# Strassen's identity for the second product of a fused attention and feed-forward kernel: seven block products for eight

## The chip, the core and the metric

The kernel runs on one core of a Trainium2 chip. Its five engines run side by side, each through its own queue in order: TensorE (PE, matmuls; its weight loads are listed as PEld), VectorE (DVE), ScalarE (ACT), GpSimd (POOL) and SyncE (SP, which here only issues transfers). TensorE writes to the accumulator memory PSUM, which has eight banks of 128 x 512 fp32 values. GpSimd and the transfers work on SBUF only. The metric is the device time of one execution in microseconds (us); the median of several runs is given. All times below are in us unless marked ns.

## The reference

There are two parts. The first is a cross attention between tokens and states, both ways, for 8 batches, 8 heads, 512 tokens, 32 states and a head width of 64. The second is a feed-forward layer over all 8 x (512 + 32) = 4352 rows, in width 512, hidden width 2048.

```python
scores = scale * np.matmul(x, state.transpose(0, 1, 3, 2))
a = softmax(scores);  xread = np.matmul(a, state)
scores2 = scale * np.matmul(state, x.transpose(0, 1, 3, 2))
a2 = softmax(scores2);  sread = np.matmul(a2, x)
attn = np.concatenate([xread, sread], axis=2)   # heads joined to rows of 512
h = attn @ w_in
g = np.maximum(0.01 * h, h)
out = g @ w_out
```

Inputs and output are fp32; the kernel multiplies in bf16 and adds in fp32.

## The kernel before, in words

The order of the work on every engine is the order of the program: it is written out by hand, with no planner, and each engine's queue runs in that order, held only by waits for data and for free buffers.

The tokens' first product is folded. For a batch, `a_m` multiplies the states with w_in in four column groups of 512 to a matrix M, so that `ff1` gets a block of 128 hidden columns for all 512 tokens from two matmuls (M as weights, the probabilities aT moving, 512 columns). ACT applies the leaky ReLU from one of two PSUM banks ("ph") into hT, which holds 16 blocks of 128 hidden columns by 512 tokens in bf16.

The second product is done in pieces. `piece(b, hT, i, jq)` adds four matmuls (128 tokens by 512 columns of w_out, one weight tile of hT each) to a bank ("py"); four pieces finish 128 tokens, and `y_store` copies the bank to SBUF and issues a transfer of 256 KB.

Batches 0 and 1 have openings of their own. Batches 2 to 7 each have a stage of 16 steps (the loop `for b in range(2, B)`). Step s runs `ff1` for hidden block s, then what the step's branch holds, then one piece: at steps 0 to 9 the rest of batch b - 1, at 10 to 15 the first three quarters of two token tiles of batch b. A matmul of ff1 can start only when the activation two blocks before has left its bank. The branches prepare the next batch, called nxt:

- step 0: SP issues the load of x[b+2] (`load_x`, 1 MB) and the transposition of the state-side probabilities (`a_a2t`).
- step 1: TensorE computes the scores of nxt and M's column group 3 for b. VectorE takes row maxima, spreads them and subtracts (`a_shift`), then column maxima (`a_max2`). Pool casts x[b+2] to bf16 (`cast_x`).
- steps 5 to 7: ACT's exponentials (`a_exp`, `a_exp2`), and VectorE's sums, reciprocals and scalings (`a_probs`, `a_probs2`).
- step 8: the states' read (`a_sread`), which needs the transposition of step 0.
- step 10: M's column groups 0, 2 and 1 of nxt; VectorE evicts 0 and 2, ACT evicts 1.
- step 13: SP issues the transposition of x[b+2] (`a_xt_dma`), which the scores need at step 1 of the next stage.

Stage 2 also loads the states of batches 4 to 7 (`load_state(1)`, step 4) and prepares them (`state_t(1)`, step 8: a cast on Pool, a transposition issued by SP). All of SP's issues are in order: a transfer whose data is late holds those behind it.

PSUM holds two banks each for "ph" and "py", and two double banks, "sc" and "big": "sc" serves scores and an M group, "big" serves M groups and the states' read.

The tail is after stage 7. `ff1_s` computes the hidden rows of the 256 state tokens (four matmuls of 256 columns per block), between the last pieces of batch 7; then come the states' second product (eight pieces) and `last_tile`, the last 128 tokens of batch 7 in two halves of 256 columns. The profile's line numbers are those of the listing below: L346 is ff1, L374 a piece, L357 ff1_s, L400 last_tile, L325 a_m, L204 the scores, L339 and L337 evictions of M, L246 the last product of a_probs, L283 the scaling of a_probs2, L104 the cast of x, L98 its load, L188 and L175 and L290 the transpositions of x, of the states and of a2.

Of the kernel before, what the change touches and what calls it, by code (L numbers as in the profile page):

```python
# [9 lines left out]
P = 128  # L10
B, H, S, D = 8, 8, 512, 64
# [16 lines left out]
def kernel(  # L28
# [14 lines left out]
    att = ctx.enter_context(tc.tile_pool(name="att", bufs=2))  # L43
    mpool = ctx.enter_context(tc.tile_pool(name="mpool", bufs=2))
    hpool = ctx.enter_context(tc.tile_pool(name="hpool", bufs=2))
    ypool = ctx.enter_context(tc.tile_pool(name="ypool", bufs=4))
    psum = ctx.enter_context(tc.tile_pool(name="psum", bufs=2, space=bass.MemoryType.PSUM))

    ENG = mybir.EngineType
# [44 lines left out]
    xs, xl = {}, {}  # L94

    def load_x(b, eng):
        xl[b] = xpool.tile([P, H, NT * D], FP32, name="xl", tag="xl", bufs=2)
        eng.dma_start(xl[b][:], x[b].rearrange("h (p t) d -> p h (t d)", t=NT))  # L98

    def open_xb(b):  # L100
# [2 lines left out]
    def cast_x(b, h0, h1, copy):  # L103
        copy(  # L104
            xs[b][:, :, h0:h1].rearrange("p t h d -> p h t d"),
            xl[b][:, h0:h1].rearrange("p h (t d) -> p h t d", t=NT),
        )
# [110 lines left out]
        return m1  # L218

    def block_sub(flat, m1, n):  # L220
        m1b = att.tile([P, n, NS], FP32, name="mrowb", tag="mrowb")
        nc.vector.transpose(m1b[:], m1[:, :, None].to_broadcast([P, n, NS]))  # L222
        sh = att.tile([P, n * NS], FP32, name="sh", tag="sh")
        nc.vector.tensor_tensor(  # L224
            out=sh[:], in0=flat, in1=m1b[:].rearrange("p c j -> p (c j)"), op=ALU.subtract,
        )
        return sh

    def block_exp(sh, n):
        e1 = att.tile([P, n * NS], BF16, name="e1", tag="e1")  # L230
        nc.scalar.activation(out=e1[:], in_=sh[:], func=AF.Exp, scale=SCALE)  # L231
        return e1

    def block_probs(dst, e1, n):
        r1 = att.tile([P, n], FP32, name="r1", tag="r1")
        nc.vector.tensor_reduce(  # L236
            out=r1[:], in_=e1[:].rearrange("p (c j) -> p c j", j=NS),
            axis=AX.X, op=ALU.add, apply_transpose=True,
        )
        nc.vector.tensor_scalar(out=r1[:], in0=r1[:], scalar1=1e-9, scalar2=None, op0=ALU.add)  # L240
        q1h = att.tile([P, n], BF16, name="qh", tag="qh")
        with nc.allow_low_precision(reason="one rounding, of the finished reciprocal"):
            nc.vector.reciprocal(q1h[:], r1[:])
        q1b = att.tile([P, n, NS], BF16, name="qb", tag="qb")
        nc.vector.transpose(q1b[:], q1h[:, :, None].to_broadcast([P, n, NS]))  # L245
        nc.vector.tensor_tensor(  # L246
            out=dst, in0=e1[:].rearrange("p (g s) -> p g s", g=2),
            in1=q1b[:].rearrange("p (g c) j -> p g (c j)", g=2), op=ALU.mult,
        )
# [38 lines left out]
    def a_a2t(a):  # L288
        a.a2T = att.tile([P, 2, NT, P], BF16, name="a2T", tag="a2T")
        nc.sync.dma_start_transpose(  # L290
            a.a2T[:].rearrange("p g i q -> p (g i) q"), a.a2[:].rearrange("p g s -> p (g s)")
        )

    def a_sread(a):
        ps = psum.tile([P, NK, 2, NS], FP32, name="psr", tag="big", bufs=1)
        for k in range(NK):
            for i in range(NT):
                nc.tensor.matmul(  # L298
                    ps[:, k, :, :],
                    lhsT=a.xb[:, i, 2 * k:2 * k + 2, :].rearrange("p h d -> p (h d)"),  # L300
                    rhs=a.a2T[:, :, i, NS * k:NS * (k + 1)],
                    start=(i == 0), stop=(i == NT - 1),
                )
        for g in range(2):
            nc.scalar.copy(
                sr_t[D * g:D * (g + 1), :, NS * a.b:NS * (a.b + 1)],
                ps[D * g:D * (g + 1), :, g, :],
            )
# [72 lines left out]
    def y_store(b, i, copy):  # L381
# [6 lines left out]
        else:  # L388
            nc.sync.dma_start(rows_of(b)[i], ysb[:])

    def rows_of(b):
        return out[b * SROW:b * SROW + S, :].rearrange("(p t) f -> t p f", t=NT)

    def last_tile(b, hT, i):
        n = DM // 2
        for half, copy in ((0, VEC), (1, SCA)):
            cols = slice(n * half, n * (half + 1))
            py = psum.tile([P, n], FP32, name="pyh", tag="py")
            for j in range(16):
                nc.tensor.matmul(  # L400
                    py[:], lhsT=hT[:, j, P * i:P * (i + 1)], rhs=w_out_bf[:, j, cols],
                    start=(j == 0), stop=(j == 15),
                )
            ysb = ypool.tile([P, n], FP32, name="ysh", tag="ysb")
            copy(ysb[:], py[:])  # L405
            nc.sync.dma_start(rows_of(b)[i][:, cols], ysb[:])

    att_of = [Attn() for _ in range(B)]
    a0, a1, a2 = att_of[:3]
# [249 lines left out]
    for s in range(16):  # L663
        ff1(a1, h1, s)
        if s % 2:
            pb, hT, i, jq = fill[s // 2]
            piece(pb, hT, i, jq, copy=VEC if s == 3 else SCA)
        if s == 4:
            a_scores(a2)
            m_evict(a2, 0, a_m(a2, 0, "big"), SCA)  # L670
            a_shift(a2)
            a_max2(a2)
        elif s == 7:
            a_exp(a2)
            a_open(att_of[3], 3)
            a_xt_dma(att_of[3])
        elif s == 8:
            a_sread(a0)
        elif s in (9, 11):
            a_exp2(a2, s // 2 - 4)  # L680
            if s == 9:
                a_probs(a2)
            else:
                a_probs2(a2)
        elif s == 13:
            a_probs2(a1)
            a_a2t(a1)
            pm = [a_m(a2, 1, "big"), a_m(a2, 2, "sc")]
            m_evict(a2, 1, pm[0], VEC)
            m_evict(a2, 2, pm[1], SCA)  # L690

    h_prev = h1
    for b in range(2, B):
        hT = hpool.tile([P, 16, S], BF16, name="hT", tag="hT")
        a = att_of[b]
        nxt = att_of[b + 1] if b + 1 < B else None
        order = [(b - 1, i, 3) for i in range(2)]
        order += [(b - 1, i, jq) for i in range(2, NT) for jq in range(4)]  # L700
        order += [(b, i, jq) for jq in range(3) for i in range(2)]
        for s in range(16):
            ff1(a, hT, s)
            if s == 0:
                if b + 2 < B:
                    load_x(b + 2, nc.sync)
                    open_xb(b + 2)
                a_a2t(a)
            elif s == 1:
                if nxt is not None:  # L710
                    a_scores(nxt)
                m_evict(a, 3, a_m(a, 3, "big"), SCA)
                if nxt is not None:
                    a_shift(nxt)
                    a_max2(nxt)
                if b + 2 < B:
                    cast_x(b + 2, 0, 8, POO)
            elif s == 4:
                if b == 2:
                    load_state(1)  # L720
            elif s == 6:
                if b == 2:
                    a_sread(a1)
            elif s == 8:
                a_sread(a)
                if b == 2:
                    state_t(1)
            if nxt is not None:
                if s == 5:
                    a_exp(nxt)  # L730
                elif s in (6, 7):
                    a_exp2(nxt, s - 6)
                    if s == 7:
                        a_probs(nxt)
                        a_probs2(nxt)
                elif s == 10:
                    pm0 = a_m(nxt, 0, "big")
                    pm2 = a_m(nxt, 2, "phpy")
                    pm1 = a_m(nxt, 1, "sc")
                    m_evict(nxt, 2, pm2, VEC)  # L740
                    m_evict(nxt, 0, pm0, VEC)
                    m_evict(nxt, 1, pm1, SCA)
                if s == 13 and b + 2 < B:
                    a_open(att_of[b + 2], b + 2)
                    a_xt_dma(att_of[b + 2])
            pb, i, jq = order[s]
            piece(pb, hT if pb == b else h_prev, i, jq)
        h_prev = hT

    hs = hpool.tile([P, 16, B * NS], BF16, name="hs", tag="hs", bufs=1)
    b = B - 1
    order = [(0, 3), (1, 3), (2, 0), (2, 1), (2, 2), (2, 3)]
    for s in range(8):
        ff1_s(hs, 2 * s)
        ff1_s(hs, 2 * s + 1)
        if s < 6:
            piece(b, h_prev, *order[s])
        else:  # L760
            piece(B, hs, 0, s - 6)
    for jq in range(2, 4):
        piece(B, hs, 0, jq)
    for jq in range(4):
        piece(B, hs, 1, jq)
    last_tile(b, h_prev, 3)


# [28 lines left out]
```

## Time and profile before

| what | value |
|---|---|
| median of 3 runs | 219.07 us (219.03 to 219.18) |
| span of the profiled execution, first to last instruction | 216.9 us |
| the profiled execution's own time | not listed; span and median differ by 2.17 us |
| granted TensorE clock | 1.000 in the mean |
| busy: PE, ACT, DVE, POOL | 96%, 63%, 46%, 10% of the span |
| transfers | 27.70 MB, of which 17.30 read and 8.91 written in main memory |
| the costliest group: pieces of tokens (L374) | 443 matmuls, 379 ns each as listed |

Three things help in reading it. The duration listed for one matmul includes its passage through the array, and matmuls overlap, so the rate is read from the distance between starts. A group's line gives the line, the engine, the operation, output and inputs by the program's names, shapes, count, then busy time and the mean of one, then the idle time of that engine just before it and what ended it. The timeline lists start, duration, engine and operation, with neighbours of one kind merged.

The stages, by the first matmul of ff1 in the timeline: batch 2 from 54.75 us, 3 from 77.94, 4 from 100.66, 5 from 123.38, 6 from 146.10, 7 from 168.84, the tail from 190.48; the last matmul ends at 213.2. TensorE is busy in nearly every moment of these stages. Stage 2 is longer than the others by one states' read (of batch 1), stage 7 shorter, since it has no next batch. VectorE is busy 12.0 us of a stage, ACT 15.7, Pool 1.9.

### The profile page before, as it was taken

What the parts mean: (1) busy time and instruction counts of PE and PEld (TensorE: products, weight loads), DVE (VectorE), ACT (ScalarE), POOL (GpSimd) and SP (SyncE); (2) the same over time, 40 slices, a digit from 0 to 9 for tenths busy, and PEclk for the clock granted to TensorE, in tenths of its full rate; (3) what the DMA queues carried; (4) which work ended last, traced back from release to release, by engine and by line L of the source; (5) the groups of instructions that cost most, each with busy time, mean ns of one, the idle gap of its engine ahead of it and who ended that gap; (6) DMA issues with size and microseconds to landing.
All of it is one profiled execution on the core that took longest, in us unless ns stands there. A gap on an engine that the chain in (4) does not pass through costs nothing.

```text
span 216.9 us, 3693 instructions
## 1 busy us (share of the span) xinstructions
PE 207.3 (96%) x1481; PEld 98.0 (45%) x1508; DVE 99.3 (46%) x153; ACT 136.8 (63%) x259; POOL 22.8 (10%) x38
## 2 busy tenths in 40 slices
PE   7899999969999999999999999999999999999993
PEld 2543434334454444444454445444444445466562
DVE  1768598698466427840966086706672000000000
ACT  3469566768868566865696478747784756464320
POOL 8830002030031002001200030000000000000000
PEclk9999999999999999999999999999999999999999
DMA  5999993993892992179214851352012110111122
GB/s 176 224 206 290 208 285 68 223 301 73 229 200 81 159 252 76 51 160 227 97 51 114 234 138 53 83 110 100 34 60 51 51 62 35 48 51 48 48 62 87
DMA packets 39888, 27.70 MB, mean 128 GB/s; under 512 B 24512, under 2 KB 35136, under 8 KB 39872
## 3 DMA queue, kind: packets, MB, share of 16 engines
q1 hardware_dynamic: 34944, 21.04, 38.3%
q0 software_dynamic: 4784, 6.29, 14.3%
q8 instruction: 12, 0.20, 0.4%
q10 hardware_dynamic: 144, 0.13, 0.4%
q14 instruction: 4, 0.03, 0.1%
HBM read 17.30 MB, written 8.91 MB: 121 GB/s over the span
## 4 chain that ended last, share of the span: by engine, by line
PE 92%; DMA 3%; DVE 2%; issue 1%; ACT 1%; ACTq 0%
PE py L374 49%; PE ph L346 21%; PE pm L325 4%; PE ph L357 3%; DMA a2T<-a 3%; PE pyw L374 3%; PE pspin L131 2%; PE ph L572 2%; PE psr L298 2%; PE pyh L400 2%; PE sc L204 1%; PE php L572 1%; DVE M L339 1%; ACT xT L435 1%; PE pxth L428 1%
## 5 line engine op out<-in xcount | busy, mean ns | idle before, releaser
L374 PE MATMUL py<-w_out_bf,hT 128*128 128x512 bf16 x443 | 116.5, 379 | 1.1
L351 ACT ACTIVATE hT<-ph 128x512 bf16<-128x512 f32 x112 | 66.7, 601 | 41.8 <-PE ph L346 41.8
L374 PEld LDWEIGHTS <-hT 128*128 128x128 bf16 x496 | 46.8, 98 | 57.1 <-issue 5.3
L346 PE MATMUL ph<-aT,M 128*128 128x512 bf16 x223 | 65.6, 379 | 0.1
L346 PEld LDWEIGHTS <-M 128*128 128x128 bf16 x224 | 21.7, 98 | 26.6 <-issue 0.8
L383 ACT COPY ysb<-py 128x512 f32<-128x512 f32 x30 | 17.6, 586 | 10.5 <-PE py L374 10.5
L214 DVE TRANSPOSE_TENSOR_REDUCE mrow<-sc 128x32 f32<-128x1024 f32 x7 | 8.8, 1250 | 33.0 <-PE sc L204 33.0
L405 DVE COPY ysh<-pyh 128x256 f32<-128x256 f32 x1 | 0.4, 425 | 47.7 <-PE pyh L400 47.7
L104 POOL CAST xb<-xl 128x2048 bf16<-128x2048 f32 (+1 forms) x6 | 10.5, 1751 | 79.3 <-DMA xl<-in_x_dram 57.8
L339 ACT CAST M<-pm 128x1024 bf16<-128x1024 f32 x13 | 13.2, 1013 | 1.9 <-PE pm L325 1.5
L236 DVE TRANSPOSE_TENSOR_REDUCE r<-e 128x32 f32<-128x1024 bf16 x7 | 8.7, 1243 | 9.6 <-ACT e L231 9.6
L339 DVE CAST M<-pm 128x1024 bf16<-128x1024 f32 x9 | 11.0, 1217 | 1.5 <-PE pm L325 1.5
L272 ACT ACTIVATE e<-sc,mcols 128x512 bf16<-128x512 f32 x16 | 11.2, 703 | 0.0
L337 DVE CAST M<-pm 128x512 bf16<-128x512 f32 x12 | 7.7, 685 | 6.3 <-PE pm L325 6.3
L264 DVE TENSOR_REDUCE mcol<-sc 128x2 f32<-128x1024 f32 x8 | 9.7, 1214 | 0.0
L361 ACT ACTIVATE hs<-ph 128x256 bf16<-128x256 f32 x16 | 6.0, 384 | 4.6 <-PE ph L357 4.4
L222 DVE STREAM_TRANSPOSE mrowb<-mrow 128x1024 f32<-128x1024 f32 x7 | 8.7, 1246 | 0.2
L245 DVE STREAM_TRANSPOSE qb<-qh 128x1024 bf16<-128x1024 bf16 x7 | 8.7, 1245 | 0.2
L224 DVE TENSOR_TENSOR sh<-sc,mrowb 128x1024 f32<-128x1024 f32 x7 | 8.6, 1224 | 0.2
L357 PE MATMUL ph<-sr_t,w_in_bf 128*128 128x256 bf16 x64 | 8.3, 273 | 0.0
L231 ACT ACTIVATE e<-sh 128x1024 bf16<-128x1024 f32 x7 | 7.4, 1050 | 1.1 <-DVE sh L224 1.1
L580 ACT ACTIVATE hT<-ph 128x512 bf16<-128x512 f32 x12 | 6.4, 598 | 2.1 <-PE ph L572 1.8
(97 smaller groups left out, 154.2 us busy)
## 6 DMA issues: line engine op xcount, KB each, us to landing
out_dram<-ysb SPq DMA_DIRECT2D x31, 256.0 KB, 2.3
xl<-in_x_dram SPq DMA_DIRECT2D x5, 1024.0 KB, 6.5
w_in_bf<-in_moe_w_in_dram POOLq DMA_DIRECT2D x4, 512.0 KB, 9.3
w_out_bf<-in_moe_w_out_dram POOLq DMA_DIRECT2D x4, 512.0 KB, 16.9
xf<-in_x_dram SPq DMA_DIRECT2D x2, 512.0 KB, 5.1
x<-in_x_dram POOLq DMA_DIRECT2D x2, 512.0 KB, 14.0
xl<-in_x_dram POOLq DMA_DIRECT2D x1, 1024.0 KB, 18.8
out_dram<-ysb SPq DMA_DIRECT2D x8, 64.0 KB, 1.7
```

What stands on the lines that cost most here:

```text
L104: copy(xs[b][:, :, h0:h1].rearrange("p t h d -> p h t d"), xl[b][:, h0:h1].rearrange("p h (t d) -> p h t d", t=NT),)
L214: nc.vector.tensor_reduce(out=m1[:], in_=flat.rearrange("p (c j) -> p c j", j=NS), axis=AX.X, op=ALU.max, apply_transpose=True,)
L222: nc.vector.transpose(m1b[:], m1[:, :, None].to_broadcast([P, n, NS]))
L236: nc.vector.tensor_reduce(out=r1[:], in_=e1[:].rearrange("p (c j) -> p c j", j=NS), axis=AX.X, op=ALU.add, apply_transpose=True,)
L264: nc.vector.tensor_reduce(out=m2[:], in_=a.sc[:], axis=AX.X, op=ALU.max, negate=True)
L272: nc.scalar.activation(out=a.e2[:, g], in_=a.sc[:, g, :], func=AF.Exp, bias=a.m2s[:, g:g + 1], scale=SCALE, accum_out=a.r2[:, g:g + 1],)
L339: copy(a.M[:, :, cols], pm[:])
L346: nc.tensor.matmul(ph[:], lhsT=a.M[:, g, P * j:P * (j + 1)], rhs=a.aT[:, g, :], start=(g == 0), stop=(g == 1),)
L351: nc.scalar.activation(out=hT[:, j, :], in_=ph[:], func=AF.Prelu, alpha=0.01)
L357: nc.tensor.matmul(ph[:, :n], lhsT=w_in_bf[:, k, P * j:P * (j + 1)], rhs=sr_t[:, k, :], start=(k == 0), stop=(k == NK - 1),)
L374: nc.tensor.matmul(y.py, lhsT=hT[:, j, P * i:P * (i + 1)], rhs=w_out_bf[:, j, :], start=(j == 0), stop=(j == 15),)
L383: copy(ysb[:], ys[b, i].py)
```

## The change

The second product of batches 2 to 7, and that of the state tokens, is cut into 2 by 2 blocks. The tokens of a batch are split in two halves of 256, the hidden width in even and odd blocks of 128 (k), and the output columns in two halves of 256. Strassen's identity (in Winograd's form) then needs seven block products in place of eight. Products 1 and 2 use blocks of hT and w_out as they are; 3 to 7 use sums of blocks on one side or both.

- Four sums of blocks of w_out ("tw") are made once, in bf16, on Pool: eight operations of 4 x 256 elements per partition with two inputs each. The first four come in batch 1's stage after step 8, the second four at step 1 of stage 2, behind the cast of x[4]. Their tiles take over the space of the first loads of x.
- Four sums of blocks of hT ("su") are made per batch on DVE, 8 x 256 elements per partition each: sums 0 and 1 in two halves (step 11 of the batch's own stage, step 0 of the next), 2 at step 3 and 3 at step 6.
- A unit is two matmuls of 128 tokens by 256 columns. A product is eight units, a batch 56. The ten first units are run at the end of a batch's own stage (OWN), 46 in the next: three or four a step.
- Products share two banks. 1, 6 and 7 add up in one; 2 is alone in the other; 5 and 3 add up there after it; 4 is alone in the first. ACT saves the bank after 1, 6, 5 and 7 (128 x 512, fp32). DVE joins: an output quarter is the bank plus a saved one, after 2, 3 and 4. Pool adds the saved 7 and 5 for the fourth.
- The output goes out in two transfers of 512 KB per batch, each of 2 rows (4 KB) per partition, after the joins of 3 and 4.
- Column maxima (a_max2) move from step 1 to step 3. M's column group 2 moves from step 10 to step 13, from the banks "ph" and "py" to "big", and its eviction from DVE (two of 512) to ACT (one of 1024).
- To make room, xl (the landing buffer of x) goes from two buffers to one, and so do mrowb, sh, e1 and qb; ysb goes from four to three. The state tokens' hidden rows hs take a buffer of hT.
- The tail runs ff1_s with one or two units of batch 7 at each block, then the seven products of the state tokens (units of one matmul), with up to four units of batch 7 after each of the first six. The state tokens' product 4 is last; its two halves of rows go out in four transfers each (out_s).

```diff
+    def weights_sums(m0, m1):
+        ms = slice(m0, m1)
+        for dst, u, v, op in (
+            (0, B12, B11, ALU.subtract), (2, B22, B12, ALU.add),
+            (1, B11, tw[2], ALU.subtract), (3, tw[1], B21, ALU.add),
+        ):
+            nc.gpsimd.tensor_tensor(
+                out=tw[dst][:, ms], in0=u[:, ms], in1=v[:, ms], op=op
+            )
...
+        def sums(self, n, m0=0, m1=NM, eng=None):
...
+            u, v, op = (
+                (A[2, 1], A[2, 2], ALU.subtract), (S[0], A[1, 1], ALU.subtract),
+                (A[2, 1], A[1, 1], ALU.subtract), (A[1, 2], S.get(1), ALU.add),
+            )[n]
...
+                (eng or nc.vector).tensor_tensor(out=S[n][:, ms], in0=u[:, ms], in1=v[:, ms], op=op)
...
+        def unit(self, bank, n, m, first):
...
+            for i in range(self.sub):
+                nc.tensor.matmul(
+                    bank[:, i, :], lhsT=lhs[:, m, P * i:P * (i + 1)], rhs=rhs[:, m, :],
+                    start=(first and m == 0 and i == 0), stop=(m == NM - 1),
...
+        def done(self, n, bank):
+            f = self.f
+            if n in (1, 6, 5, 7):
+                f.save(n, bank)
+            if n == 2:
+                f.join(self.yo(0)[:, :, :HC], bank, 1)
+            elif n == 7:
+                nc.gpsimd.tensor_tensor(
+                    out=self.yo(1)[:, :, HC:], in0=f.sv[7][:], in1=f.sv[5][:], op=ALU.add
+                )
+            elif n == 3:
+                f.join(self.yo(0)[:, :, HC:], bank, 6)
+                self.out(0)
+            elif n == 4:
+                f.join(self.yo(1)[:, :, :HC], bank, 7)
+                self.out(1)
...
         elif s == 8:
             a_sread(a0)
+            weights_open()
+            weights_sums(0, 4)
...
                 a_a2t(a)
+                if before:
+                    for n in (0, 1):
+                        before.f.sums(n, 4, 8)
             elif s == 1:
                 if nxt is not None:
                     a_scores(nxt)
                 m_evict(a, 3, a_m(a, 3, "big"), SCA)
                 if nxt is not None:
                     a_shift(nxt)
-                    a_max2(nxt)
                 if b + 2 < B:
                     cast_x(b + 2, 0, 8, POO)
+                if b == 2:
+                    weights_sums(4, 8)
+            elif s == 3:
+                if before:
+                    before.f.sums(2)
+                if nxt is not None:
+                    a_max2(nxt)
...
+            if s == 11:
+                for n in (0, 1):
+                    now.f.sums(n, 0, 4)
...
-                    pm2 = a_m(nxt, 2, "phpy")
                     pm1 = a_m(nxt, 1, "sc")
-                    m_evict(nxt, 2, pm2, VEC)
                     m_evict(nxt, 0, pm0, VEC)
                     m_evict(nxt, 1, pm1, SCA)
+                elif s == 13:
+                    m_evict(nxt, 2, a_m(nxt, 2, "big"), SCA)
...
-            piece(pb, hT if pb == b else h_prev, i, jq)
...
+            n = 3 + s % 2 if b > 2 else 2
+            left = len(before.units) if before else 0
+            if left:
+                before.run(min(n, left))
+            if n > left:
+                now.run(min(n - left, OWN - own))
```

## The prediction

> **What bounds the kernel now.** I read the shares of busy time first, then the chain that ended last, then the timeline of each engine around one batch.
>
> ```profile
> PE 207.3 (96%) x1481; PEld 98.0 (45%) x1508; DVE 99.3 (46%) x153; ACT 136.8 (63%) x259; POOL 22.8 (10%) x38
> ...
> PE 92%; DMA 3%; DVE 2%; issue 1%; ACT 1%; ACTq 0%
> ```
>
> TensorE is busy 96% and is 92% of the chain: in the stages of batches 2 to 7 it never waits, so time comes off only where TensorE has less to do, and every new wait of TensorE is paid in full. The end of the chain in order of time (start, duration) gives the price of a narrow matmul, and the timeline that of a wide one:
>
> ```profile
> 202.80 0.87 PE ph L357 x8
> ...
> 209.71 3.51 PE pyh L400 x32
> ```
> ```profile
> 185.73 1.03 PE L374 MATMUL py<-w_out_bf,hT 128*128 128x512 bf16 x4
> 186.59 0.59 PE L346 MATMUL ph<-aT,M 128*128 128x512 bf16 x2
> ```
>
> Eight of 256 columns take 0.87, 32 take 3.51: 0.109 each, a new weight tile with each. Four of 512 take 186.59 - 185.73 = 0.86: 0.2155 each. Rates of the other engines (min/median/max ns, and groups with mean ns):
>
> ```profile
> L104 POOL CAST xb<-xl x6: 1040/1893/1894, 34.5 to 125.7; 128x2048 bf16<-128x2048 f32 x5, 128x1024 bf16<-128x1024 f32 x1
> ```
> ```profile
> L111 DVE CAST xb<-xf x2: 427/618/808, 5.4 to 7.0; 128x512 bf16<-128x512 f32 x2
> ...
> L111 POOL CAST xb<-xf x1: 609/609/609, 7.0 to 7.0; 128x512 bf16<-128x512 f32 x1
> ```
> ```profile
> L246 DVE TENSOR_TENSOR aT<-e,qb 128x1024 bf16<-128x1024 bf16 x7 | 4.9, 704 | 0.2
> ...
> L383 DVE COPY ysb<-py 128x512 f32<-128x512 f32 x1 | 0.7, 692 | 1.2 <-PE py L374 1.2
> ```
>
> Pool needs 0.833 ns per element that it reads, and 0.19 more. The same DVE cast took 0.43 alone and 0.81 at 7.03, when Pool's own cast held from 6.95 to 7.56. Last, the queues around batch 2 (SyncE, VectorE, Pool):
>
> ```profile
> 53.30 1.23 SPq L290 DMA_TRANSPOSE a2T<-a  x1
> 54.63 0.53 SPq L98 DMA_DIRECT2D xl<-in_x_dram  x1
> ...
> 67.36 1.19 SPq L175 DMA_TRANSPOSE st_t<-stb  x1
> 70.10 0.36 SPq L389 DMA_DIRECT2D out_dram<-ysb  x1
> 70.52 3.67 SPq L188 DMA_TRANSPOSE xT<-xb  x1
> ```
> ```profile
> 49.86 0.69 DVE L246 TENSOR_TENSOR aT<-e,qb 128x1024 bf16<-128x1024 bf16 x1
> ...
> 53.19 1.22 DVE L339 CAST M<-pm 128x1024 bf16<-128x1024 f32 x1
> ```
> ```profile
> 62.12 1.89 POOL L104 CAST xb<-xl 128x2048 bf16<-128x2048 f32 x1 [15.73 <-DMA xl<-in_x_dram]
> 66.72 0.61 POOL L174 CAST stb<-stf 128x512 bf16<-128x512 f32 x1 [2.72 <-DMA stf<-in_state_dram]
> ```
>
> SyncE issues in order: the state's transposition waits for Pool's cast of it, and the transposition of x[4] stands behind that.
>
> **The sum's base.** The profiled execution has a span of 216.9; the median of the three runs is 219.07, so 2.17 lies around the span. I keep that and add changes to 219.07.
>
> **TensorE's work.** A batch's second product was 64 x 0.2155 = 13.79; seven products of 8 x 2 narrow matmuls are 112 x 0.109 = 12.21. Batch 2's stage (54.75 to 77.94) held 16 pieces; now 10 pieces and 20 narrow matmuls, 8.62 + 2.18: -2.99. In the stages of 3 to 6: -1.58 each. M's column group 2 goes to a place of its own at step 13, one more gap of 0.09 as before the other group starts: batch 2 -2.90, 3 to 6 -1.49 x 4 = -5.96, batch 7 -1.58. The tail held 64 narrow (6.98), 6 pieces (5.17), 8 pieces of the states (6.90) and 32 narrow (3.49), 22.54; now 6.98 + 92 x 0.109 (10.03) + 56 x 0.109 (6.10) = 23.11: +0.57. Sum -9.87.
>
> **DVE in the stages of 3 to 6.** It was busy 12.0 of 22.7. Out: two copies of M, 1.37. In: sums of 4 x 1024 and 2 x 2048 bf16 elements, by L246 (start to start 0.61, and twice the elements 1.14) 4.7; three joins of 512 at 0.69, 2.1. Some 17.5 of a stage of 21.2: it fits on average, so what counts is order. Let t be 0 at the first matmul of a stage. Scores at step 1 let the row maximum start at t = 2.10 (ff1 of step 1 at 1.09, plus 102.97 - 101.96); the three operations up to the subtraction take 3.70 (102.97 to 106.67). The join of product 2 is queued behind them: 5.80 to 6.49. TensorE reaches product 5, which starts over that bank, at step 4: 5 x 0.431 + 14 units x 0.218 + 0.65 (scores and M) = 5.86. It waits to 6.55: 0.69 in each of four stages, +2.76 (not in batch 7, which has no next batch). Bounds: 0, if the scores' chain starts earlier, and 1.4, if the join costs twice the copy that prices it. Behind it all meets: third sum done at 10.2, needed at 12.2; join 3 at 17.3, needed at 18.8; join 4 at 19.7, needed at 21.0. The halves of sums 0 and 1 at step 0 wait for the last activation and are done by 1.4, ahead of the scores.
>
> **ACT.** Four copies out (0.586), four saves of the same size in, one copy of M (1.01) more: 16.7 of 21.9 busy. Each save has a whole product of 1.7 before its bank is used again: 0. The activations' own reserve is the two banks of ff1, which a late exponential would use up first.
>
> **SyncE and DMA in later stages.** Two outputs of 512 KB for four of 256 KB. The first goes after join 3 (t = 17.3), the transposition of x[b+2] behind it lands 4.8 later (4.3 to 5.8), at 22 to 23.5, needed at 23.5: 0, with almost no reserve. The load of x[b+2], now one buffer, goes behind the second output at about 21, casts by t = 7 of the next stage, needed by step 13: 0. The tiles that go from two buffers to one (row maxima spread, shifted scores, exponentials, reciprocals) are each read within the stage that writes them, the last read by t = 15 and the next write after t = 23: 0.
>
> **The end.** From the last matmul to the end it is 3.7 (213.2 to 216.9), 3.2 of it from the last DMA's issue. Now three groups queue on SyncE: four row DMAs of the first state tile from 0.75 before the last matmul's end (0.42 each, median), batch 7's output (0.35), four more: the last goes at 2.54, so 5.74: +2.0. Bounds 0 and 3.
>
> **The weight sums on Pool, the term that decides.** Eight operations of 1024 elements with two inputs. No such row; bounds are 1.04 (one element per read cycle, the 1024 cast) and two reads, 0.19 + 2 x 0.853 = 1.89. I take 1.89: both inputs must be read. The Trainium skill (GPSIMD Engine Reference, section 3.1) has 4.5 for 2048 elements with two inputs, so an estimate of 2.3 here, and the sum would be some 3 later; no run here shows it.
> The L111 rows say that a DVE operation meeting a Pool operation waits for its end: 0.81 is the rest of Pool's 0.53 plus 0.43, less 0.15. I count that wait as whole, and let the engines alternate. Bounds: nothing, or the whole of the Pool operation each time. The Trainium skill (SBUF - State Buffer, Who interferes with whom) calls it an exclusive lock for the whole instruction, also for DVE operations with two SBUF inputs; by that rule, the trace agrees.
> First four: Pool is free at 46.4 and starts them there. L246 goes from 49.86 to 50.4, the scalings of a2 wait to 53.0 and 55.1, and the cast of M at 53.19 starts at 56.5 and ends at 57.7. Its bank is wanted at 56.79: TensorE waits 1.0. The transposition of a2 (53.30) is issued at 56.6, the load of x[4] behind it at 57.9 instead of 54.63, so Pool's cast moves from 62.12 to 65.4.
> Second four: queued behind that cast, from 67.4, alternating with L240, L246 and the scalings: done at 76.4. The state's cast 77.1, its transposition's issue 78.3, the output 78.7, x[4] lands at 83.5. Scores of batch 4 stand at step 1 of batch 3: 77.94 - 2.90 + 1.60 = 76.64 without any wait. All waits on the way are inside this one: +6.9. The longest wait of TensorE in the trace is 1.7, at a granted clock of 1.00; whether the clock holds over 4 to 5 it does not show, and I price that at 0.
>
> **Sum.** 219.07 - 9.87 + 2.76 + 2.0 + 6.9 = 220.9.
>
> **Rivals.**
> Faster, Pool is quick: at 1.04 the first four are over at 50.8, nothing is late, the second four end at 68.9, x[4] lands at 75.9, before 76.64. Then 214.0. For it: Pool has little else to do. Against: two inputs. It is decided at about 1.7 per operation, where the wait eats the 5.1 gained.
> Faster, no blocking: at 1.89 the second four run from 64.0 to 71.7, x[4] lands at 78.7: +2.1, 216.1. Against: 0.43 to 0.81.
> Slower, DVE is the bound: if the sums, over strided blocks, run at the rate of L224 (1024 in 1.22), each batch gets 4.3 more, 22 of 21.9; join 4 comes after it is wanted, about 1 a stage: 225. Against: L246 also reads two bf16 inputs, in rows of 512.
> The change doesn't do what it says: above 13.79/112 = 0.123 a narrow matmul saves nothing, and it ends near 230. Against: 0.109 in L357 and L400.
>
> **How the numbers follow.** Forecast as worked out 0.58, own range 218.8 (a price near 1.7) to 224 (the end at its bound, +1, and x[b+2] late by 0.5 in four stages, +2); quick Pool 0.13; no blocking 0.17; both faster cases with 1 to either side; DVE bound 0.08; no saving 0.04. Within 0.2% (0.44, what a measurement of this kernel can tell from no change): a band of the forecast's lower end, 0.05. Faster: 0.13 + 0.17 + 0.03 of the forecast's low end = 0.33; slower 0.62. The range 213.5 to 224 leaves out the two last cases and a rest of the first rival.
>
> **What would show it.** Narrow products at 0.109; Pool's sums near 1.9 and DVE operations stretched beside them; a wait of TensorE for the DMA of xT in batch 3 of 3 to 5; four waits of 0.7 for the join at step 4; 5.7 after the last matmul. It is wrong if Pool's sums are near 1, if DVE beside them keeps its durations, or if xT is in time.

## The result: slower by 2.2%

The changed kernel takes 223.98 us (median of 4 runs, 223.65 to 224.14), the kernel before 219.08 on the same chip. The ratio is 1.0221, with a 95% interval of 1.0206 to 1.0236: 4.9 us lost where the forecast lost 1.8. The profiled execution took 223.65 with a span of 221.9, against 216.9 before: 5.0 in span. The chips of the later experiments had the kernel before at 219.1 to 219.2, so their times are compared directly. The ratios leave out a few executions that were over 1.5% slower than the fastest of the same kernel, and they are not formed from the medians, so they can differ by some 0.3% from the quotient of the medians.

The page of the changed kernel, shares of busy time and the chain that ended last:

```profile
PE 202.4 (91%) x1804; PEld 127.3 (57%) x1804; DVE 151.0 (68%) x205; ACT 142.2 (64%) x266; POOL 48.9 (22%) x53
...
PE 44%; DVE 25%; DMA 17%; POOL 5%; issue 5%; SPq 1%; POOLq 0%; DVEq 0%
```

TensorE is busy 4.9 less than before, but it is 44% of the chain and no longer 92%: the other engines and the transfers are now most of it. What TensorE waits for in the changed kernel (total, number of waits, longest):

```profile
PE pm L326 <- DVE M L340: 2.7, 1, 2.7
PE ph L347 <- ACT hT L352: 2.6, 2, 2.1
PE py L375 <- DVE ysb L384: 2.3, 1, 2.3
PE yq L446 <- DVE yo L458: 2.0, 4, 0.5
PE sc L205 <- DMA xT<-xb: 1.5, 3, 0.8
```

By the first matmul of each stage in the two timelines, the 5.0 lie as follows.

| part | before | after | change |
|---|---|---|---|
| ahead of stage 2 | 54.75 | 58.01 | +3.26 |
| stage 2 | 23.19 | 24.54 | +1.35 |
| stages 3 to 6 | 90.90 | 89.82 | -1.08 |
| stage 7 | 21.64 | 20.04 | -1.60 |
| tail, to the end of the last matmul | 22.72 | 23.31 | +0.59 |
| from there to the end | 3.7 | 6.18 | +2.48 |

**Ahead of stage 2**, where nothing was forecast, lie the second and the third line of the waits. The timeline of VectorE, then of TensorE:

```profile
45.29 0.69 DVE L384 COPY ysb<-py 128x512 f32<-128x512 f32 x1 [6.05 <-DMA out_dram<-ysb]
45.90 1.24 DVE L215 TRANSPOSE_TENSOR_REDUCE mrow<-sc 128x32 f32<-128x1024 f32 x1
```
```profile
46.04 1.02 PE L375 MATMUL py<-w_out_bf,hT 128*128 128x512 bf16 x4 [2.32 <-DVE ysb L384]
51.37 0.59 PE L347 MATMUL ph<-aT,M 128*128 128x512 bf16 x2 [2.11 <-ACT hT L352]
```

VectorE is idle for 6.05 ahead of its copy of an output of batch 0, until the transfer of an earlier output has read its buffer: ysb has three buffers where it had four. In the kernel before, the same copy starts at 40.39 after an idle time of 1.24, which TensorE ends. The row maxima of batch 2 queue behind that copy, and TensorE stops for the copied bank and then twice for an activation (2.11, and 0.44 at 52.40). The waits of 1.74 for a2T and of 0.41 for x that the kernel before has in this stretch are gone: 2.32 + 2.11 + 0.44 - 1.74 - 0.41 = 2.72 of the 3.26.

**Stage 2** holds the weight sums. Pool's timeline, then VectorE's:

```profile
68.81 2.12 POOL L410 TENSOR_TENSOR tw_xf<-w_out_bf 128x1024 bf16<-128x1024 bf16 x1
70.89 2.57 POOL L410 TENSOR_TENSOR tw_x<-w_out_bf 128x1024 bf16<-128x1024 bf16 x1
73.54 2.13 POOL L410 TENSOR_TENSOR tw_xf<-w_out_bf,tw_x 128x1024 bf16<-128x1024 bf16 x1
75.74 2.12 POOL L410 TENSOR_TENSOR tw_x<-tw_xf,w_out_bf 128x1024 bf16<-128x1024 bf16 x1
77.80 0.67 POOL L175 CAST stb<-stf 128x512 bf16<-128x512 f32 x1
```
```profile
69.34 1.25 DVE L246 STREAM_TRANSPOSE qb<-qh 128x1024 bf16<-128x1024 bf16 x1
...
71.40 2.08 DVE L279 TENSOR_SCALAR r<-r 128x2 f32<-128x2 f32 x1
...
73.72 4.29 DVE L284 TENSOR_SCALAR a<-e,qc 128x512 bf16<-128x512 bf16 x2
77.93 1.21 DVE L340 CAST M<-pm 128x1024 bf16<-128x1024 f32 x1
```

The same operations 14 to 16 us earlier in the same timeline, with no sum on Pool:

```profile
57.02 0.16 DVE L279 TENSOR_SCALAR r<-r 128x2 f32<-128x2 f32 x1
...
57.42 0.62 DVE L284 TENSOR_SCALAR a<-e,qc 128x512 bf16<-128x512 bf16 x2
```

An operation on two columns that takes 0.16 alone takes 2.08 beside Pool, and two that take 0.62 together take 4.29: each ends within 0.2 of the end of a Pool sum (73.48 and 73.46, 78.01 and 77.86). A transposition of 1024 elements (1.25) beside the sums takes what it takes alone (1.25 at 55.13). The cast of M is queued behind them, so TensorE waits, and then runs slowly. TensorE's timeline, and four windows of 1.2 us (busy time of PE, PEld, DVE, ACT and POOL, then the granted clock, the share of the DMA engines and GB/s):

```profile
79.19 0.63 PE L326 MATMUL pm<-w_in_bf,st_t 64*32 64x512 bf16 x8 [2.67 <-DVE M L340]
85.01 0.41 PE L205 MATMUL sc<-xT,st_t 64*32 64x512 bf16 x8 [0.78 <-DMA xT<-xb]
```
```profile
79.20:80.40 1.20, 1.20 (x12) 0.58 (x12) 1.17 (x2) 0.52 (x1) 0.00 (x0) 0.50 0.53 109
80.40:81.60 1.20, 1.20 (x5) 0.58 (x4) 0.06 (x1) 0.50 (x1) 0.00 (x0) 0.50 0.67 190
81.60:82.80 1.20, 1.20 (x9) 0.71 (x7) 0.00 (x0) 0.64 (x2) 0.00 (x0) 0.86 1.05 209
82.80:84.00 1.20, 1.20 (x10) 0.75 (x8) 0.62 (x1) 1.20 (x3) 0.00 (x0) 1.00 1.12 206
```

For 3 us after the wait the clock is at 0.50 to 0.86 and TensorE does 1.2 x (0.50 + 0.50 + 0.14) = 1.37 less. Wait and clock are 4.0; without them stage 2 is 20.5, 2.7 shorter than before.

**At the end** SyncE still issues for 3.7 after the last matmul's end (215.72). Its timeline:

```profile
214.97 1.75 SPq L918 DMA_DIRECT2D out_dram<-yhs  x4
216.83 0.36 SPq L480 DMA_DIRECT2D out_dram<-yo  x1
217.30 2.12 SPq L918 DMA_DIRECT2D out_dram<-yhs  x4
```

### The profile page after: what moved, and what is told of

The parts are those of the page before. It is cut to its first block, busy times and chain, and to the rows that moved or that the text cites. A ratio compares the mean times of both kernels' runs of the same rounds, so it can differ in the third digit from the quotient of the medians.

```text
span 221.9 us, 4381 instructions
## 1 busy us (share of the span) xinstructions
PE 202.4 (91%) x1804; PEld 127.3 (57%) x1804; DVE 151.0 (68%) x205; ACT 142.2 (64%) x266; POOL 48.9 (22%) x53
## 4 chain that ended last, share of the span: by engine, by line
PE 44%; DVE 25%; DMA 17%; POOL 5%; issue 5%; SPq 1%; POOLq 0%; DVEq 0%
PE yq L446 19%; PE ph L347 8%; DMA xT<-xb 7%; DMA w_in_bf<-in_moe_w_in_dram 5%; PE pyw L375 3%; PE ph L358 3%; DMA out_dram<-ysb 3%; DVE mrowb L223 3%; DVE mrow L215 3%; DMA xl<-in_x_dram 3%; DVE su L435 3%; PE py L375 2%; DVE M L340 2%; POOL tw_xf L410 2%; DVE aT L247 2%
## 5 line engine op out<-in xcount | busy, mean ns | idle before, releaser
L446 PEld LDWEIGHTS <-su 128*128 128x128 bf16 x416 | 40.0, 98 | 16.5 <-issue 4.8
L446 PE MATMUL yq<-tw_xf,su 128*128 128x256 bf16 x192 | 27.6, 272 | 2.0 <-DVE yo L458 2.0
L446 PE MATMUL yq<-w_out_bf,hT 128*128 128x256 bf16 x192 | 27.3, 278 | 0.0
L375 PE MATMUL py<-w_out_bf,hT 128*128 128x512 bf16 x96 | 24.2, 379 | 2.3 <-DVE ysb L384 2.3
L435 DVE TENSOR_TENSOR su<-hT 128x1024 bf16<-128x1024 bf16 (+1 forms) x18 | 16.6, 924 | 12.1 <-ACT hT L352 12.1
L458 DVE TENSOR_TENSOR yo<-yq,sv 128x512 f32<-128x512 f32 x18 | 12.3, 686 | 16.6 <-PE yq L446 16.6
L340 ACT CAST M<-pm 128x1024 bf16<-128x1024 f32 x18 | 18.2, 1011 | 5.0 <-PE pm L326 4.9
L455 ACT COPY sv<-yq 128x512 f32<-128x512 f32 x24 | 14.0, 585 | 3.3 <-PE yq L446 3.2
L446 PE MATMUL yq<-tw_x,hT 128*128 128x256 bf16 x96 | 13.5, 273 | 0.0
L446 PE MATMUL yq<-w_out_bf,su 128*128 128x256 bf16 x96 | 13.5, 273 | 0.0
L446 PE MATMUL yq<-tw_x,su 128*128 128x256 bf16 x96 | 13.4, 273 | 0.0
```

The costliest lines, as they stand in the source:

```text
L340: copy(a.M[:, :, cols], pm[:])
L375: nc.tensor.matmul(y.py, lhsT=hT[:, j, P * i:P * (i + 1)], rhs=w_out_bf[:, j, :], start=(j == 0), stop=(j == 15),)
L435: (eng or nc.vector).tensor_tensor(out=S[n][:, ms], in0=u[:, ms], in1=v[:, ms], op=op)
L446: nc.tensor.matmul(bank[:, i, :], lhsT=lhs[:, m, P * i:P * (i + 1)], rhs=rhs[:, m, :], start=(first and m == 0 and i == 0), stop=(m == NM ...
L455: copy(t[:], bank)
L458: nc.vector.tensor_tensor(out=dst, in0=bank, in1=self.sv[n][:], op=ALU.add)
```

## The experiments

Two causes were in question: Pool's sums, as forecast, and the buffer taken from ysb, which the forecast had not priced. The first runs ask whether both carry a share (A), or the buffer (B) or the sums (C) carry it alone. The edits below are to the changed kernel where nothing else is said.

**1. A fourth place for batch 0's outputs.** The second output tile of batch 0 goes to the space of the later output tile yo0.

```diff
+        if (b, i) == (0, 1):
+            ysb = ypool.tile([P, 2, DM], FP32, name="yo0", tag="yo0", bufs=1)[:, 0, :]
+        else:
+            ysb = ypool.tile([P, DM], FP32, name="ysb", tag="ysb")[:]
...
```

> The second output tile of batch 0 gets a buffer of its own, so that three ysb buffers do what four did; all else as changed. Theory A (two causes, each hiding a part of the other: the wait of DVE's copy for an output transfer, 6.05, and Pool's sums that block DVE and hold up the transposition of x[4]): TensorE's waits of 2.3 and 2.1 in batch 1's stage go, but Pool's first four sums, 2.12 each, then hold DVE's scalings and the cast of M instead; scores of batch 4 come about 2 earlier: 222.0. Theory B (the buffer alone): the whole 8.3 by which the scores of batch 4 are late goes: 215.7. Theory C (Pool's sums alone): 224.0, no change.

Measured: 221.01 (220.97 to 221.70), ratio to the kernel before 1.0077 [1.0028, 1.0126]. The buffer is worth 3.0 us, 1.0 more than theory A expected. TensorE no longer waits for ysb. What remains is the wait for M in two places (1.28 at the start of stage 2, 2.70 at its end), and the wait for a2T is back:

```profile
PE pm L326 <- DVE M L340: 4.0, 2, 2.7
...
PE psr L299 <- DMA a2T<-a: 1.8, 1, 1.8
```

**2. The weight sums on VectorE**, all eight, in the same places of the order.

```diff
-            nc.gpsimd.tensor_tensor(
-                out=tw[dst][:, ms], in0=u[:, ms], in1=v[:, ms], op=op
-            )
+            with nc.allow_low_precision(reason="operands of a product"):
+                nc.vector.tensor_tensor(
+                    out=tw[dst][:, ms], in0=u[:, ms], in1=v[:, ms], op=op
+                )
```

> All eight weight sums on DVE, at the same places of the program, in place of Pool; three ysb buffers as changed. Each should take 0.7 on DVE. Theory A: the wait for the output transfer stays, stage 2 still begins at 58.0, but then runs without waits of TensorE for M and for x[4] and without the half clock after them: scores of batch 4 near 80.2 instead of 85.0: 219.2. Theory B: 224 or more, as DVE has 5 more to do. Theory C: 215.7.

Measured: 220.04 (218.68 to 222.22, 10 runs), ratio 1.0041 [1.0013, 1.0068]; 3.9 less than the changed kernel. Each sum takes 0.69 on VectorE. The wait for M is gone, the wait of 2.5 for ysb stands, and so does the one of 2.1 for an activation behind it.

**3. Both.**

> Both: the second output tile of batch 0 in a buffer of its own, and the eight weight sums on DVE. Theory A: stage 2 begins near 54.8, the scores of batch 4 stand near 76.8: 215.7, with the later stages and the tail as changed. Theory B or C alone: the same 215.7, reached by one of the two edits. Rival D (the seven products do not pay on TensorE, the waits are only where the loss shows): 219 or above.

Measured: 216.25 (214.38 to 216.89), ratio 0.985 [0.9796, 0.9904]. The two causes add up within the spread of the runs (3.0 + 3.9 = 6.9, against 7.7 for both), and the kernel is now faster than before: both causes are real, and nearly apart from each other. That a VectorE too full is behind this loss is excluded, since it carries more work here than in the changed kernel. VectorE's timeline shows one sum that still meets Pool's cast of x, then Pool's:

```profile
62.84 0.68 DVE L414 TENSOR_TENSOR tw_x<-w_out_bf 128x1024 bf16<-128x1024 bf16 x1
63.55 2.38 DVE L414 TENSOR_TENSOR tw_xf<-w_out_bf,tw_x 128x1024 bf16<-128x1024 bf16 x1
```
```profile
63.50 1.89 POOL L105 CAST xb<-xl 128x2048 bf16<-128x2048 f32 x1 [17.22 <-DMA xl<-in_x_dram]
```

The cast begins 0.05 earlier and ends at 65.39; the sum ends 0.54 after it. Alone it takes 0.69, so at most 0.15 of it was done while Pool ran.

**4. Pool's order.** The second four sums go behind the state cast, from step 1 to step 8 of stage 2. This parts two effects of the sums: the queue on Pool in front of the state cast (and so of x[4]'s transposition), and the blocking of VectorE.

```diff
-                if b == 2:
-                    weights_sums(4, 8)
             elif s == 3:
...
                     state_t(1)
+                    weights_sums(4, 8)
```

> Pool's second four weight sums are put behind the cast of the states of batches 4 to 7 (step 8 instead of step 1 of stage 2), still on Pool; all else as changed. If what counts is SyncE's queue (x[4]'s transposition behind the states' behind Pool's sums): scores of batch 4 no longer wait for x[4], and the half clock may still come: about 222.5. If what counts is DVE blocked by Pool (scalings, then the cast of M that frees a bank for TensorE at step 13): the 2.67 wait for M stays and the gain is under 1: 223.2. If both count: about 221.

Measured: 223.06 (ratio 1.0159 [1.0104, 1.0214]), 0.9 less than the changed kernel, and its runs spread from 221.2 to 223.5, so here the trace decides and not the time. The queue is gone: x[4]'s transposition is issued at 75.85 in place of 80.37, and the scores of batch 4 wait for nothing. But the blocking has moved to the sums of hT. VectorE's timeline, and TensorE's:

```profile
76.20 2.52 DVE L435 TENSOR_TENSOR su<-hT 128x1024 bf16<-128x1024 bf16 x1
78.75 2.49 DVE L435 TENSOR_TENSOR su<-su,hT 128x1024 bf16<-128x1024 bf16 x1
81.17 2.61 DVE L435 TENSOR_TENSOR su<-hT 128x1024 bf16<-128x1024 bf16 x1
83.81 0.69 DVE L435 TENSOR_TENSOR su<-su,hT 128x1024 bf16<-128x1024 bf16 x1
```
```profile
88.85 0.81 PE L446 MATMUL yq<-tw_xf,su 128*128 128x256 bf16 x6 [2.72 <-DVE yo L458]
```

0.69 becomes 2.5 three times, and TensorE waits 2.72 for the join of product 2, where it waits 0.49 in the changed kernel. So the time is the one expected for blocking (223.2), but not by the wait that was named: the wait for M is gone. The blocking is enough by itself to cost the time; taking the queue away alone doesn't win it back.

Runs 5 to 7 each add one edit to run 3, for the smaller terms.

**5. The join of product 2 ahead of the spread of the row maxima**, with the units of step 1 run before the subtraction.

```diff
-                if nxt is not None:
+                if nxt is not None and before:
+                    flat = nxt.sc[:].rearrange("p g c -> p (g c)")
+                    m1 = block_max(flat, NB)
+                    early = min(4, len(before.units))
+                    before.run(early)
+                    nxt.sh = block_sub(flat, m1, NB)
+                elif nxt is not None:
                     a_shift(nxt)
...
+            if s == 1 and before and nxt is not None:
+                n = left = 0
```

> On top of both edits (own buffer, weight sums on DVE: 216.25): at step 1 of stages 3 to 6 DVE gets the join of product 2 right after the row maxima, ahead of the spread and the subtraction, and not behind them. If the four waits of TensorE for that join (2.2 in sum) are on the path: 214.0. If the subtraction that comes 0.6 later delays the exponential and with it ff1's activations: 216 or above.

Measured: 214.89 (213.06 to 216.20), ratio 0.982 [0.9779, 0.9862]: 1.36 less than run 3, with overlapping intervals, so the trace has to decide. All four join waits are gone, 2.2 in run 3. Part of that came back as a longer wait for x[b+2] (1.2 in two places, where run 3 has 0.6).

**6. x[b+2]'s transposition issued at step 9** instead of 13 in stages 3 to 5.

```diff
-                if s == 13 and b + 2 < B:
+                if s == (13 if b == 2 else 9) and b + 2 < B:
```

> On top of both edits: in stages 3 to 5 SyncE issues the transposition of x[b+2] at step 9, ahead of the batch's first output, instead of step 13 behind it. If its landing is what the scores wait for at step 1 (0.6 in one stage of the kernel with both edits, 1.5 in three stages of the changed one): 215.6. If SyncE or the transfers then hold up the output or the next load: no gain, 216.2.

Measured: 216.2 (214.44 to 217.75), ratio 0.9834 [0.9785, 0.9882]: nothing gained in the median. The execution that was profiled is the slowest of the four: its wait for a2T ahead of stage 2 is 2.79, where run 3 has 2.05. The wait that the edit aims at, 0.59 for x at the scores of stage 4 in run 3, is gone from its trace; one of 0.38 stands in stage 3, whose transposition has not moved. What that is worth can't be read from this run; run 10 takes the question up again.

**7. Half of the last row transfers from ScalarE's queue.**

```diff
-            nc.sync.dma_start(out[r0:r0 + NS, :], ysb[i][NS * bb:NS * (bb + 1), 0, :])
+            (nc.scalar if bb % 2 else nc.sync).dma_start(
+                out[r0:r0 + NS, :], ysb[i][NS * bb:NS * (bb + 1), 0, :]
+            )
```

> On top of both edits: of each four row transfers of the state tokens every second is issued from ACT's queue, idle by then, the others from SyncE. If the end is held by SyncE's nine issues in a row (the last one 2 us after TensorE's last result is joined): 214.5. If it is held by the transfers' own bandwidth: 216.2.

Measured: 215.39 (214.71 to 216.07), ratio 0.9823 [0.9787, 0.986]. From the last matmul's end to the end it is 5.39, where run 3 has 6.13: 0.74 of the 0.86 between the medians, and less than half of the 1.75 that was expected.

**8. All of these edits together.**

> All of these together: own buffer, weight sums on DVE, join ahead of the spread, transposition of x[b+2] at step 9, the state tokens' rows from two queues. If the terms are independent waits they add: 211.8, of which TensorE's work alone gives 219.1 - 9.9 = 209.2 and the rest is the end. If DVE is near its bound in these stages they add less: 213.5.

Measured: 213.48, ratio 0.973 [0.9679, 0.9782], with runs from 212.06 to 214.38. The number is that of the branch "VectorE near its bound", but it doesn't show that: runs 5 to 7 gained 1.36, 0.05 and 0.86 one by one, 2.3 in sum, and together they gain 2.8 over run 3. They add; each was expected to be larger. TensorE's longest wait is now the one for a2T, 2.78. It is in the kernel before too (1.74), so it is not new with the change.

**9. All edits, and the states' read of batch 0 two steps later** (step 10 of batch 1's stage), behind the arrival of a2T.

```diff
         elif s == 8:
-            a_sread(a0)
             weights_open()
             weights_sums(0, 4)
+        elif s == 10:
+            a_sread(a0)
```

> The version with all the edits, and batch 0's attention row a2T now read into the first product two steps later in batch 1's stage (step 10, not 8), where its transposed copy is already there. Nothing of the computation is left out. If TensorE's long wait in stage 1 (2.78 us in the version with all the edits) and the half clock that sometimes follows such waits are a cost of their own: 213.5 less about 2, that is about 211.3 us, with a smaller spread between runs, and no wait over 1 us in stage 1. Rival: what ends that wait is ready no earlier for the rest of the stage, so another wait takes its place and the time stays at 213.5.

Measured: 211.68 (211.27 to 212.21), ratio 0.9633 [0.9574, 0.9693]. The wait went and no long one took its place. What TensorE waits for in this run, longest first after the warm-up:

```profile
PE pm L326 <- DVE M L340: 0.6, 1, 0.6
PE ph L347 <- ACT hT L352: 0.5, 1, 0.5
PE sct L561 <- DVE xT L553: 0.3, 1, 0.3
```

**10. Run 9 without the earlier issue of x[b+2]'s transposition** (the text below says load; the load stays where it is).

> The same as the run with the later read, but the load of the next batch's x issued where the changed kernel has it. If SyncE's reserve is really used up (waits of 0.4 to 1.2 us for x at the start of stages 4 to 6), the time is about 1 us longer than in that run, some 212.3 us. If the earlier issue was worth nothing, as when it was tried alone (216.2 against 216.25), the two agree within 0.3 us.

Measured: 213.25 (211.94 to 214.02), ratio 0.9697 [0.9616, 0.9777]. The intervals of runs 9 and 10 overlap, but the two profiles show where the 1.57 lies. TensorE's timeline of run 10:

```profile
98.89 0.41 PE L205 MATMUL sc<-xT,st_t 64*32 64x512 bf16 x8 [0.73 <-DMA xT<-xb]
...
142.64 0.41 PE L205 MATMUL sc<-xT,st_t 64*32 64x512 bf16 x8 [0.81 <-DMA xT<-xb]
```

0.73 + 0.81 = 1.54, and neither stands in run 9. So by the traces the reserve of that transfer was used up, and worth about 1.5 once nothing else covered it.

**11. Run 9 with the weight sums back on Pool.**

> The same as the run with the later read, but the eight weight sums back on Pool, as in the changed kernel. If a Pool sum of 2.12 us holds up VectorE's steps beside it and the state cast behind it, the 4.8 us between the first and the third run return, or most of them: about 216 us, with a wait for M of over 2 us at the start of stage 2. Rival: the other edits have given VectorE enough time to hide them, and it is at about 212 us.

Measured: 218.85 (216.82 to 220.45), ratio 0.9956 [0.9919, 0.9993]. The rival (212) falls: by this single edit the sums on Pool cost 7.2 us, more than the 4.8 between runs 1 and 3. Run 3 has losses of its own that run 9 does not have (2.05 for a2T, 1.7 by the clock at half behind it, 0.59 for x), which make the difference between runs 1 and 3 the smaller one. TensorE's waits in run 11:

```profile
PE pm L326 <- DVE M L340: 3.8, 3, 2.5
PE sc L205 <- DMA xT<-xb: 1.8, 2, 1.4
...
PE psr L299 <- DMA a2T<-a: 1.2, 1, 1.2
```

These are 6.2 more than run 9 has of the same kinds (0.6), and the clock after the longest (1.00, 0.59, 0.50 and 0.50 in windows of 1.2 us) takes 1.7: 7.9 in sum, where the spans differ by 7.7.

**12. The kernel before with that later read** (its step 10 in place of 8).

> The kernel before with only the later read of batch 0's attention row (step 10 in place of 8), the fair base for the version that has it. Its own wait of 1.74 us in stage 1 goes, nothing is at half clock there: about 217.2 us. Rival: a later step of stage 1 waits in its place, 219.1 us as before.

Measured: 217.79 (217.25 to 218.06, 10 runs), ratio 0.9919 [0.9892, 0.9947]. Its wait for a2T (1.74) is gone, and one of 0.40 for an activation is new. So 1.35 of the gain of run 9 has nothing to do with Strassen's identity. Against this base run 9 is at 211.68/217.79 = 0.972: the identity itself, with the time lost beside it won back, is worth 6.1 us. Whether the other edits, the two queues for the last rows above all, would also help the kernel before was not tried.

## Why the prediction was right or wrong

The sign was right, the size wrong: +4.9 measured, +1.8 forecast; 223.98 lies just inside the upper end of the forecast's range.

| step of the forecast | forecast | shown |
|---|---|---|
| narrow matmul of 256 columns | 0.109 | 0.109 |
| TensorE's work, stage 2 | -2.90 | -2.7 (without wait and clock) |
| TensorE's work, stages 3 to 6, each | -1.49 | -1.35, -0.84, -1.35 (run 9, start to start of the scores: 21.37, 21.88, 21.37) |
| stage 7; tail | -1.58; +0.57 | -1.60; +0.59 |
| wait for the join of product 2, each | 0.69 | 0.66 (stage 5: 134.40, where 133.31 + 0.43 was due; 0.49 of it listed as idle) |
| VectorE in a stage of 3 to 6 | some 17.5 | 18.2 to 19.1, busy in 22.0 to 22.5 |
| one weight sum on Pool | 1.89 | 2.12 to 2.57 |
| from the last matmul to the end | 5.74 | 6.18 |
| wait for x at the scores of batch 4 | 3 to 5 | 0.78; none in run 1 |
| x[b+2] in later stages | 0 | 0.36, 0 and 0.40 |
| tiles with fewer buffers | 0 | 3.0 (run 1) |
| clock after a long wait | 0 | 1.37 |

**The step that failed: "The tiles that go from two buffers to one".** It listed mrowb, sh, e1 and qb, and priced them at nothing by the last read within a stage. ysb, from four buffers to three, was not on its list, although the change names it. With the step's own rule (last read of the old content against the next write) the answer stood in the trace of before (two lines of VectorE's timeline, one of SyncE's, and the transfers of 30 to 48 us):

```profile
36.94 1.29 DVE L383 COPY ysb<-pyw 128x512 f32<-128x512 f32 x2 [0.85 <-PE pyw L374]
...
40.39 0.69 DVE L383 COPY ysb<-py 128x512 f32<-128x512 f32 x1 [1.24 <-PE py L374]
```
```profile
38.95 1.05 SPq L389 DMA_DIRECT2D out_dram<-ysb  x2
```
```profile
out_dram<-ysb SPq DMA_DIRECT2D x4, 256.0 KB, 6.2
```

The four copies start at 36.94, 37.5, 38.66 (on ACT) and 40.39, a buffer each, and the reader of the first is a transfer that SyncE issues only at 38.95, behind a load of x and a transposition. From issue to landing the four outputs of that stretch take 6.2 (median), so a fourth copy in three buffers starts at about 38.95 + 6.2 = 45.15, not at 40.39; it started at 45.29. With the place given back (run 1), the time is 221.01, where the forecast had 220.9. That agreement is in part luck, because a second step had the wrong path (next paragraph): the forecast has the scores of batch 4 at 83.5, where they wait for x; run 1 has them at 82.92, with no wait for x. The end and the gaps were priced too low.

**The term that decided was right in kind.** Pool's sums do block VectorE, and rivals one and two (Pool is quick; no blocking) fall: 2.12 is above both the 1.89 taken and the point of 1.7. The estimate of 2.3 that the forecast worked out from the Trainium skill (GPSIMD Engine Reference, section 3.1) was nearer than the 1.89 that it took; the measurement decides for 2.12. The counting was too simple in one respect: "a DVE operation meeting a Pool operation waits for its end" holds for the operations that the traces stretch (L279, L284 and L247 in part, and in run 4 the sums of hT), not for the transpositions and the reads of PSUM, which took 1.25 and 1.22 beside Pool's sums. The Trainium skill (SBUF - State Buffer, Who interferes with whom) limits the lock to operations of VectorE with two SBUF inputs or in a mode that uses both ports. The rows agree for the two-input sums (0.69 to 2.5), and no run here shows the modes themselves.

**The path was wrong: "All waits on the way are inside this one".** The forecast put the whole cost of Pool's sums on one wait of TensorE, for x at the scores of batch 4. Its wait of 1.0 for M behind the first four sums is hidden by the late stage in the changed kernel, and stands at 1.28 in run 1. But the second four met the scalings of a2, so that TensorE paid first for M at the end of stage 2 (2.67), which the forecast didn't have, and then only 0.78 for x[4]. In run 1 there is no wait for x[4] left: 1.28 and 2.70 for M and 1.70 by the clock behind the second make 5.7, in place of the forecast's 6.9. By the forecast's own sign ("if xT is in time") that step fails.

**Clock.** The forecast saw a wait of 1.7 at a clock of 1.00 and priced longer ones at nothing. 2.67 lost 1.37.

**Rivals three and four** fall: VectorE at 18.2 to 19.1 is not the bound of a stage, and the narrow matmul saves what it should.

**Stays open**: why each of stages 3 to 6 is some 0.15 longer than the sum has it (22.02 less 22.72 in stage 5 is -0.70, by the sum -1.49 + 0.66 = -0.83), and why one of run 9's stages gains 0.5 less than its neighbours (a wait of 0.29 for a sum of hT is part of that). No run was made for it.

## What to carry to other kernels

When a change takes buffers away to make room, go through every tile whose count falls, and ask of each who reads it last; where that is a transfer, the price is in the DMA queue, not on an engine. Before work is put on an idle Pool, list what VectorE does in that stretch: in this case sums of two SBUF tensors and scalings stopped until Pool's operation was over, while transpositions and reads of PSUM did not, and VectorE, filled to 68% but three times as fast at these sums (0.69 against 2.12), was still the better place. Take one cause away at a time, but judge small ones again at the end, when no larger wait covers them: the transfer whose earlier issue showed no gain in run 6 was worth 1.5 in run 10.

## What was not expected of the hardware

The granted clock can fall to 0.50 after a wait of TensorE of only 2 to 3 us, for about 3 us. All waits of over 1.5 us ahead of a matmul, over the profiles of this case:

| wait of TensorE, us | granted clock in the windows of 1.2 us after it |
|---|---|
| 1.55, 1.74, 1.81, 1.90 | 1.00 each time |
| 2.05 (run 3) | 0.99, 0.50, 0.50, 0.58 |
| 2.11 (three profiles) | 1.00 in the changed kernel and run 4; 0.54, 0.50, 0.53 in run 2 |
| 2.32, 2.55, 3.08 | 1.00 each time |
| 2.49 (run 11) | 1.00, 0.59, 0.50, 0.50, 0.99 |
| 2.67 | 0.50, 0.50, 0.86 |
| 2.70, 2.72 | 0.88 or 0.89, 0.50, 0.50, 0.70 |
| 2.78 (run 8) | 1.00 |
| 2.79 (run 6) | 0.50, 0.50, 0.76 |

The three waits of 2.11 are the same wait, for an activation ahead of stage 2. The windows behind it in run 2, where it ends at 51.46, then in the changed kernel, where it ends at 51.37:

```profile
51.46:52.66 1.20, 1.11 (x3) 0.35 (x3) 1.09 (x3) 1.16 (x4) 0.00 (x0) 0.54 0.00 0
52.66:53.86 1.20, 1.20 (x4) 0.42 (x3) 1.17 (x3) 1.20 (x4) 0.00 (x0) 0.50 0.03 7
53.86:55.06 1.20, 1.20 (x5) 0.37 (x4) 1.17 (x2) 0.95 (x3) 0.00 (x0) 0.53 0.00 0
```
```profile
51.37:52.57 1.20, 0.76 (x3) 0.28 (x3) 1.20 (x2) 0.99 (x4) 1.12 (x2) 1.00 0.00 0
52.57:53.77 1.20, 1.20 (x6) 0.48 (x5) 1.17 (x2) 1.20 (x4) 1.20 (x1) 1.00 0.00 0
```

So the length of the wait alone doesn't decide it. The Trainium skill (TensorE: Matmul & The Clock Gate, Part 1) explains the gate by a window of about 3.4 us that runs freely, so that the moment of a change depends on where in the window the work falls. The 2.5 to 4 us of lowered clock in the rows above would fit that; no run here shows the window. The Trainium skill (TensorE: Matmul & The Clock Gate, Why this matters for your kernels) advises no gaps of over about 3 us. That is too generous for this kernel: gaps from 2.05 on cost up to 1.7 beside themselves, and 3.08 once cost nothing. The clock may be why most of the kernels with a wait of over 1.5 us spread over 2 us from run to run, while the ten runs of one without (run 12) lie within 0.8; that was not tried by itself, and run 10, whose waits are 0.8 at most, spreads over 2.1 too.
